# Attention and feed-forward in one kernel: the feed-forward steps two at a time, and x at another place in memory

## The chip, the cores and the metric

The kernel runs on one core of one Trainium2 chip. A core has a matrix engine (TensorE, PE in the profile), a vector engine (VectorE, DVE), a scalar engine (ScalarE, ACT), a general engine (GpSimd, POOL), and a sync engine (SyncE, SP) whose queue here issues every transfer. Each works through its own list of instructions in order; semaphores make one wait for another. The metric is the device time of one execution in microseconds (us), lower is better. A time is given as the median of several runs.

## What is computed

Four sequences of 768 tokens, eight heads of 64. Each query attends to the keys less than 16 places away and to 24 summaries, one for each block of 32 tokens: the maximum of the block's keys (its score raised by log 32), the mean of its values. The result, x with 512 features, goes through a feed-forward part with 2048 hidden features and a gate that is 0 below −1, h above 1 and (h + 1)²/4 between. Cut to what matters:

```python
k_sum = k.reshape(B, H, nb, block, D).max(axis=3)
v_sum = v.reshape(B, H, nb, block, D).mean(axis=3)
scores_l_m = np.where(mask_l, scale * q @ k.T, -1e9)
scores_s = scale * q @ k_sum.T + np.log(block)
a = softmax(concat([scores_l_m, scores_s]))
x = a @ concat([v, v_sum])
h = x @ w_in
g = np.where(h >= 1, h, np.where(h <= -1, 0.0, (h + 1) ** 2 / 4))
out = g @ w_out
```

## The kernel before

**Chunks, pairs and steps.** The 3072 tokens are cut into 8 chunks of 384, so a sequence is two chunks; an even chunk begins a sequence. Heads go in four pairs of 128 features. The hidden features go in 16 steps of 128 (f = 0 to 15). x, g and the two weights are each split into a high and a low half of a reduced 32-bit type (fp32r), and each product is made from three: low times high, high times low, high times high.

**A feed-forward step.** Step f of a chunk has these parts, with their letters in the code:
- F (`ff1`, L374): h, 12 products of 384 columns, whose moving operand is x. h takes one of two PSUM banks (`ps_h`).
- G, H (ACT, L380 and L386) and I (DVE, L392): the gate. I is the last reader of h and frees its bank.
- J (ACT, L397) and O (POOL, L402): the high and the low half of g. There are three buffers for the high and two for the low halves.
- B (`ff2`, L415): acc, 9 products of 512 columns, into three banks (one for each 128 tokens), over all 16 steps.
B of a step stands two steps behind its F.

**The attention between the steps.** While a chunk's 16 steps run, the attention of the next chunk is made, one pair of heads in each four steps. Ahead of every fourth step (`meet`): A, the values' product of one pair (o_ps, L350), its high and low halves X and L, then the next pair's S, the scores (s_ps, L292), mask, exponentials E and normalising. Behind the h of the last of four (`turn`): T, transposes (t_ps, L336), and P, their copies. Where the next chunk begins a sequence, the first turn of the chunk also makes Z (L267): one transpose of vsum, the sums of the values' blocks of all four pairs (vs_ps). V and W take it from there into the values.

**Loads and the shared buffers.** The raw values of a sequence (vraw, four loads of 384 KB, `load_raw_vals`, L221) are summed by DVE (Y, L249). The raw keys (kraw, L202) are reduced by DVE into ksum (R, L241). When a chunk is through, its result is copied from PSUM into three tiles o (U, L421 and L423) and stored (L427). vraw, kraw and o all have tag "w" of one pool, with three buffers in rotation: each new tile waits until the one three places earlier has been used up, a result tile's when its store has landed.

**The order.** Chunk 0 and the first few products of chunk 1 follow a list written out by hand (`OPENING`, L41 to L62). Chunks 1 to 7 follow a loop (L503 to L523) that fixes the order of PE by hand; the order of the other engines is put by a scheduler. In the loop before the change, a chunk begins: `meet`, B of step 14 of the chunk before, F of step 0, `finish` of the chunk before (B of its step 15, copies, stores), F 1, F 2, B 0, F 3, turn, B 1, and goes on with F f, B f − 2. In odd chunks the loads and sums of the next sequence's values stand in the loop ahead of F 0 (pairs 0 and 1) and ahead of F 1 (pairs 2 and 3).

**Small constants.** Three columns of constants (`ones_half`, `tiny`, `halved`) lie in spare columns of ksum.

Of the kernel before, what the change touches and what calls it, by code (L numbers as in the profile page):

```python
# [8 lines left out]
F32 = mybir.dt.float32  # L9
# [29 lines left out]
LAG = 2  # L39
# [36 lines left out]
def fused_kernel(ctx: ExitStack, tc: tile.TileContext, q2, kT, kwin, vT, vwin, w_in, w_out, mask, ident, out):  # L76
# [4 lines left out]
    stage = ctx.enter_context(tc.tile_pool(name="stage", bufs=1))  # L81
    load = ctx.enter_context(tc.tile_pool(name="load", bufs=2))
    att = ctx.enter_context(tc.tile_pool(name="att", bufs=2))
    xpool = ctx.enter_context(tc.tile_pool(name="xpool", bufs=2))
    gpool = ctx.enter_context(tc.tile_pool(name="gpool", bufs=3))
    ps_h = ctx.enter_context(tc.tile_pool(name="ps_h", bufs=2, space=PSUM))
    ps = ctx.enter_context(tc.tile_pool(name="ps", bufs=6, space=PSUM))

# [1 line left out]
    ident_sb = const.tile([P, P], F32, name="ident_sb")  # L90
    ident_up = const.tile([P, P], F32, name="ident_up") if MASK_PE else None
    ksum = const.tile([P, NPAIR, SB], F32, name="ksum")
    ones_half, tiny, halved = ksum[:, 0, NSUM:NSUM + 1], ksum[:, 0, NSUM + 1:NSUM + 2], ksum[:, 0, NSUM + 2:NSUM + 4]
    nc.vector.memset(ones_half, 0.5)
    nc.vector.memset(tiny, 1e-9)
    vsum = const.tile([P, NPAIR, SB], F32, name="vsum")
# [43 lines left out]
    def convert_join(i, at):  # L140

        step, part = divmod(at, 2)
        low, top = (word[:, part * DM:(part + 1) * DM] for word in raws[i])
        if step == 0:
            c_ps = joining[i, part] = ps.tile([P, DM], I32, tag="ps", name=f"c{i}_{part}")
            nc.vector.tensor_scalar(out=c_ps, in0=top, scalar1=3, scalar2=0x7FFFFFF8,
                                    op0=ALU.logical_shift_left, op1=ALU.bitwise_and)
        elif step == 1:
            nc.vector.scalar_tensor_tensor(out=joining[i, part], in0=top, scalar=-0x80000000, in1=joining[i, part],  # L149
                                           op0=ALU.bitwise_and, op1=ALU.bitwise_or)  # L150
        else:
            if i not in converting and i in LATE:
                converting[i] = room(i, "wide", [P, 4 * DM], F32)[:, :2 * DM].bitcast(I32)
                for n in range(2):
                    whole[pairs[i][1] + n] = converting[i][:, n * DM:(n + 1) * DM].bitcast(F32)
# [26 lines left out]
    q_ts, k_ts, v_ts, s_pss, es, dens, t_pss, pts, vs_pss, o_pss, xs = ({} for _ in range(11))  # L182
# [9 lines left out]
    for i, share in enumerate(FIRST):  # L192
        at, at_room = 0, room(NF - 1 - i, "first", [P, 4 * DM], F32)
        for what, p in share:
            shape = {"q": [NB, P], "k": [NB, KA], "v": [NB, P], "vraw": [S - T]}.get(what, [S])
# [20 lines left out]
    def load_raw_vals(c, p):  # L216


        first = T if c == 0 else 0
        v_raw = raws["v", c, p] = input_tile(stage, "vraw", [P, S - first], c, p)  # L220
        nc.sync.dma_start(out=v_raw, in_=vT[c // NHALF, p, :, first:])  # L221

    def load_vals(c, p):
        v_ts[c, p] = input_tile(load, "v", [P, NB, P], c, p)
# [19 lines left out]
        nc.gpsimd.tensor_copy(out=k_ts[c, p][:, :, KW:KA], in_=ksum[:, p, :NSUM].unsqueeze(1).broadcast_to([P, NB, NSUM]))  # L244

    def sum_vals(c, p):
        v_raw = raws["v", c, p]
        first = T // SB if c == 0 else 0
        nc.vector.tensor_reduce(out=vsum[:, p, first:NSUM], in_=v_raw.rearrange("p (n j) -> p n j", j=SB), axis=AX.X, op=ALU.add)  # L249
# [10 lines left out]
    def turn_vals(c, p):  # L260


        if c == 0:
            nc.tensor.transpose(vs_pss[c, p][:NSUM, P:2 * P], vsum[:, p, :NSUM], ident_sb)
        else:
            vs_pss[c, p] = ps.tile([P, 512], F32, tag="ps", name=f"vs_ps{c}_{p}")
            nc.tensor.transpose(vs_pss[c, p][:, :P], vsum.rearrange("p a b -> p (a b)"), ident_sb)  # L267

    def mean_vals(c, p):
# [75 lines left out]
    def values(c, p):  # L345
        o_pss[c, p] = ps.tile([P, 512], F32, tag="ps", name=f"o_ps{c}_{p}")
        for blk in range(NB):
            cols = slice(blk * QB, (blk + 1) * QB)
            for j in range(2):
                nc.tensor.matmul(o_pss[c, p][j * D:(j + 1) * D, cols], v_ts[c, p][:KA, blk, j * D:(j + 1) * D],  # L350
                                 pts[c, p, j][:KA, cols], start=True, stop=True)

    def high(c, p):
        hi = xpool.tile([P, T], F32R, tag=f"xhi{p}", name=f"xhi{c}_{p}")
        lo = xpool.tile([P, T], F32R, tag=f"xlo{p}", name=f"xlo{c}_{p}")
        if f"{c}{p}" in X_DVE:
# [12 lines left out]
    def ff1(c, f, k):  # L369
        if k == 0:  # L370
            hs[c, f] = ps_h.tile([P, 512], F32, tag="h", name=f"h{c}_{f}")
        x_hi, x_lo = xs[c, k]
        for n, (w, x) in enumerate(((1, x_hi), (0, x_lo), (0, x_hi))):
            nc.tensor.matmul(hs[c, f][:, :T], weight["win", f][w][:, k], x,  # L374
                             start=(k == 0 and n == 0), stop=(k == NK - 1 and n == 2))
# [28 lines left out]
    def ff2(c, f):  # L404
        if f == 0:
            acc[c] = [ps.tile([P, DM], F32, tag="ps", name=f"acc{c}_{i}") for i in range(NTT)]
        if c == 0 and f in whole:
            products = [(gs[c, f], whole[f])]
        else:
            (g_hi, g_lo), (w_hi, w_lo) = gs[c, f], weight["wout", f]  # L410
            products = [(g_lo, w_hi), (g_hi, w_lo), (g_hi, w_hi)]
        for i in range(NTT):
            rows = slice(i * P, (i + 1) * P)
            for n, (a, w) in enumerate(products):
                nc.tensor.matmul(acc[c][i], a[:, rows], w, start=(f == 0 and n == 0),  # L415
                                 stop=(f == NF - 1 and n == len(products) - 1))
# [34 lines left out]
    def scale_ident():  # L451
# [6 lines left out]
        "T": transposes, "P": turned, "Y": sum_vals, "z": halve_sum, "x": halve_copy, "Z": turn_vals, "V": mean_vals, "W": spread_vals, "A": values, "X": high, "L": low,  # L458
# [37 lines left out]
    def finish(c):  # L496
        do(f"B{c}{NF - 1:x} " + " ".join(f"U{c}{i} o{c}{i}" for i in range(NTT)))
# [89 lines left out]
```

## Time and profile before

| | |
|---|---|
| median of 3 runs | 657.88 us (656.59 to 659.27) |
| the profiled execution | 657.0 us |
| its span | 655.2 us |
| mean granted clock of TensorE | 0.992 of full |
| busy: PE, ACT, POOL, DVE | 97%, 56%, 40%, 38% |
| moved by DMA | 71.25 MB, 109 GB/s |

The page comes from one execution. Rows of groups give the line of the kernel, engine, operation, output and inputs, shapes, count, then busy microseconds, mean nanoseconds of one, and the idle time ahead of them with what ended it. Rows of the timeline give start and duration in microseconds and then the same names; in brackets, if the engine stood idle before, how long and for whom. Matmuls are pipelined: a product's own duration is longer than the distance to the next, so lengths of runs are read from starts. "SPq" rows are the issue of transfers, and their duration is not that of the transfer.

### The profile page before, as it was taken

How to read it: one execution, taken by the hardware profiler on the slowest of the kernel's cores; microseconds unless marked ns; L12 is line 12 of the kernel's file. 1: busy time of each engine (PE TensorE's matmuls, PEld its weight loads, DVE VectorE, ACT ScalarE, POOL GpSimd, SP SyncE). 2: the span in 40 equal slices, each digit the busy share in tenths (PEclk: the TensorE clock that was granted, in tenths of full speed). 3: DMA queues.
4: the chain of work that ended last, by engine and by line, in shares of the span. 5: the costliest groups of instructions: out<-in, count | busy, mean ns of one | idle time of the engine just before them, and what ended most of it. 6: DMA issues, size and time to landing. Idle time of an engine off the chain costs nothing.

```text
span 655.2 us, 11582 instructions
## 1 busy us (share of the span) xinstructions
PE 634.8 (97%) x4471; PEld 562.7 (86%) x4471; DVE 245.7 (38%) x473; ACT 364.8 (56%) x952; POOL 265.1 (40%) x302
## 2 busy tenths in 40 slices
PE   3999999899999999999999999999999999999997
PEld 2888888788889888888988888898888898889996
DVE  5789989452214222251222422143222222211111
ACT  5689986455455555455455544555554554544333
POOL 3579998252343332243333333234333333212221
PEclk9979999999999999999999999999999999999999
DMA  8996452542115222261223420163221110010001
GB/s 328 411 414 230 177 198 72 196 163 72 32 41 192 72 73 71 72 194 47 72 72 125 139 72 15 58 214 98 71 72 60 64 46 20 1 49 0 1 2 48
DMA packets 28167, 71.25 MB, mean 109 GB/s; under 512 B 2800, under 2 KB 3568, under 8 KB 28112
## 3 DMA queue, kind: packets, MB, share of 16 engines
q1 hardware_dynamic: 28112, 70.52, 30.7%
q8 instruction: 35, 0.57, 0.4%
q14 instruction: 20, 0.16, 0.1%
HBM read 64.21 MB, written 6.29 MB: 108 GB/s over the span
## 4 chain that ended last, share of the span: by engine, by line
PE 91%; DMA 2%; ACT 2%; DVE 1%; POOL 1%; SPq 1%; issue 1%; POOLq 0%; DVEq 0%; ACTq 0%
PE h L374 40%; PE acc L415 39%; PE o_ps L350 4%; PE s_ps L292 4%; PE t_ps L336 3%; DMA ident_sb<-in_ident 1%; DMA raw<-in_w_in 1%; PE vs_ps L255 1%; ACT t L380 0%; DVE c L149 0%; ACT e L318 0%; POOL v L276 0%; SPq L202 0%; DVE t L392 0%; ACT raw L138 0%
## 5 line engine op out<-in xcount | busy, mean ns | idle before, releaser
L374 PE MATMUL h<-xhi,halves 128*128 128x384 f32 x1024 | 285.6, 340 | 3.3 <-DVE t L392 3.3
L415 PE MATMUL acc<-halves,ghi 128*128 128x512 f32 x768 | 240.4, 394 | 0.0
L402 POOL TENSOR_TENSOR glo<-t,ghi 128x384 fp32r<-128x384 f32 x128 | 129.0, 1009 | 236.4 <-ACT ghi L397 236.4
L374 PEld LDWEIGHTS h<-xhi,halves 128*128 128x128 f32 x1024 | 187.6, 188 | 12.0 <-DVE t L392 4.4
L374 PE MATMUL h<-xlo,halves 128*128 128x384 f32 x512 | 172.1, 336 | 0.0
L392 DVE SCALAR_TENSOR_TENSOR t<-h,t 128x384 f32<-128x384 f32 x128 | 71.0, 556 | 264.8 <-ACT t L386 261.2
L415 PEld LDWEIGHTS acc<-halves,ghi 128*128 128x128 f32 x768 | 144.1, 188 | 27.9
L415 PE MATMUL acc<-halves,glo 128*128 128x512 f32 x384 | 153.2, 399 | 0.8 <-POOL glo L402 0.8
L380 ACT ACTIVATE t<-h,ksum 128x384 f32<-128x384 f32 x128 | 73.7, 578 | 118.0 <-PE h L374 116.3
L397 ACT CAST ghi<-t 128x384 fp32r<-128x384 f32 x128 | 65.6, 513 | 68.3 <-DVE t L392 68.2
L318 ACT ACTIVATE e<-e,den 128x120 f32<-128x120 f32 x192 | 73.2, 383 | 52.1 <-DVE den L307 52.0
L374 PEld LDWEIGHTS h<-xlo,halves 128*128 128x128 f32 x512 | 96.4, 188 | 4.0
L415 PEld LDWEIGHTS acc<-halves,glo 128*128 128x128 f32 x384 | 72.2, 188 | 13.7 <-POOL glo L402 1.5
L386 ACT ACTIVATE t<-t 128x384 f32<-128x384 f32 x128 | 66.8, 525 | 2.4
L331 POOL TENSOR_TENSOR e<-e,den 128x360 f32<-128x360 f32 x64 | 49.2, 787 | 41.0 <-DVE den L327 37.8
L276 POOL COPY v<-mean 24x768 f32<-24x768 f32 x30 | 24.7, 822 | 56.0 <-DMA v<-in_vwin 48.4
L179 POOL TENSOR_TENSOR halves<-w,halves 128x1024 fp32r<-128x1024 f32 x16 | 38.6, 2411 | 1.6 <-PE acc L415 0.5
L364 DVE TENSOR_TENSOR xlo<-o_ps,xhi 128x384 fp32r<-128x384 f32 x32 | 17.8, 556 | 49.1 <-ACT xhi L359 49.0
L318 ACT ACTIVATION_READ_ACCUMULATOR e<-e,den 128x1 f32 x192 | 36.0, 187 | 0.0
L350 PEld LDWEIGHTS o_ps<-pt,v 120*64 120x64 f32 x720 | 24.5, 143 | 10.7 <-issue 6.7
L303 DVE SCALAR_TENSOR_TENSOR e<-s_ps,mask_sb 128x360 f32<-128x360 f32 x64 | 30.9, 524 | 6.2 <-PE s_ps L292 5.9
L336 PE MATMUL t_ps<-ident_sb,e 128*120 128x128 f32 x192 | 29.7, 289 | 2.2 <-DMA ident_sb<-in_ident 2.1
(68 smaller groups left out, 405.9 us busy)
## 6 DMA issues: line engine op xcount, KB each, us to landing
v<-in_vwin SPq DMA_DIRECT2D x29, 384.0 KB, 3.2
q<-in_q SPq DMA_DIRECT2D x28, 384.0 KB, 4.2
k<-in_kwin SPq DMA_DIRECT2D x28, 360.0 KB, 4.6
raw<-in_w_in SPq DMA_DIRECT2D x8, 1024.0 KB, 9.7
raw<-in_w_out SPq DMA_DIRECT2D x8, 1024.0 KB, 13.2
out<-o SPq DMA_DIRECT2D x24, 256.0 KB, 2.0
kraw<-in_kT SPq DMA_DIRECT2D x13, 384.0 KB, 3.7
vraw<-in_vT SPq DMA_DIRECT2D x12, 384.0 KB, 3.7
```

The lines of the kernel that those rows point to most:

```text
L179: nc.gpsimd.tensor_tensor(out=lo, in0=converting[i].bitcast(F32), in1=hi.bitcast(F32), op=ALU.subtract)
L318: nc.scalar.activation(out=es[c, p, j][:, t, :], in_=s[:, t, :], func=AF.Exp, bias=nm[:, t:t + 1], scale=scale, accum_out=den[:, t:t + 1])
L331: nc.gpsimd.tensor_tensor(out=e, in0=e, in1=den.unsqueeze(2).broadcast_to([P, NT, KA]), op=ALU.mult)
L336: nc.tensor.transpose(t_pss[c, p, j][:KA, t * P:(t + 1) * P], es[c, p, j][:, t, :], ident_sb)
L350: nc.tensor.matmul(o_pss[c, p][j * D:(j + 1) * D, cols], v_ts[c, p][:KA, blk, j * D:(j + 1) * D], pts[c, p, j][:KA, cols], start=True, sto ...
L374: nc.tensor.matmul(hs[c, f][:, :T], weight["win", f][w][:, k], x, start=(k == 0 and n == 0), stop=(k == NK - 1 and n == 2))
L380: nc.scalar.activation(out=ts[c, f], in_=hs[c, f][:, :T], func=AF.Relu, bias=ones_half, scale=0.5)
L386: nc.scalar.square(out=ts[c, f], in_=ts[c, f])
L392: nc.vector.scalar_tensor_tensor(out=g, in0=hs[c, f][:, :T], scalar=1.0, in1=ts[c, f], op0=ALU.max, op1=ALU.min)
L397: nc.scalar.copy(out=hi, in_=ts[c, f])
L402: nc.gpsimd.tensor_tensor(out=lo, in0=ts[c, f], in1=hi.bitcast(F32), op=ALU.subtract)
L415: nc.tensor.matmul(acc[c][i], a[:, rows], w, start=(f == 0 and n == 0), stop=(f == NF - 1 and n == len(products) - 1))
```

## The change

**Pairs.** From chunk 1's loop on, PE makes two steps of h in a row (24 products), then two of acc (18 products). A group of four steps becomes meet, F F, B B, F F, turn, B B. A chunk begins: meet, B 14 and B 15 of the chunk before with its copies and stores, F 0, F 1, F 2, F 3, turn, B 0, B 1. The last chunk ends with four B in a row.

**The values' loads.** In odd chunks all four loads and sums of the next sequence's values stand behind F 1, and so behind `finish` with its three result tiles.

**Places.** The three constants move to a small tile of 64 bytes in `xpool`, and `gpool` is now created ahead of `xpool`. So the tiles of x lie 64 bytes into a block of 256; before they began such a block, as those of g and the weights did and do.

**The rest.** `full`, `X_POOL`, `F_DVE`, the key of `whole` and the full-length vraw tiles are not used by any step of this program or change no instruction, but for `HALF`, which keeps the shorter sums of chunk 0 as they were. The order of the hand-written list is unchanged on every engine.

```diff
+HALF = "02 00 01 03".split()
...
+    gpool = ctx.enter_context(tc.tile_pool(name="gpool", bufs=3))
     xpool = ctx.enter_context(tc.tile_pool(name="xpool", bufs=2))
-    gpool = ctx.enter_context(tc.tile_pool(name="gpool", bufs=3))
...
-    ones_half, tiny, halved = ksum[:, 0, NSUM:NSUM + 1], ksum[:, 0, NSUM + 1:NSUM + 2], ksum[:, 0, NSUM + 2:NSUM + 4]
+    small = xpool.tile([P, 16], F32, tag="small", name="small", bufs=1)
+    ones_half, tiny, halved = small[:, 0:1], small[:, 1:2], small[:, 2:4]
...
     with tc.manual_schedule(engines={mybir.EngineType.PE}):
         for c in range(1, NCH):
-            for f in range(NF):
+            for f in range(0, NF, 2):
                 if f % 4 == 0:
                     meet(c, NPAIR - 1) if f == 0 else meet(c + 1, f // 4 - 1)
-                    if f == 0:
-                        do(f"B{c - 1}{NF - LAG:x}")
-                s = f"{c}{f:x}"
-                if c % NHALF and c + 1 < NCH and f < 2:
-                    do(" ".join(f"y{c + 1}{p} Y{c + 1}{p}" for p in (2 * f, 2 * f + 1)))
+                if f == 0:
+                    do(f"B{c - 1}{NF - 2:x}")
+                    finish(c - 1)
+                for n in (f, f + 1):
+                    s = f"{c}{n:x}"
+                    do(f"F{s}0 F{s}1 F{s}2 F{s}3 G{s} H{s} I{s} J{s} O{s}")
+                if c % NHALF and c + 1 < NCH and f == 0:
+                    do(" ".join(f"y{c + 1}{p} Y{c + 1}{p}" for p in range(NPAIR)))
...
-                do(f"F{s}0 F{s}1 F{s}2 F{s}3 G{s} H{s} I{s} J{s} O{s}")
-                if f % 4 == 3 and c + 1 < NCH:
+                if f % 4 == 2 and c + 1 < NCH:
                     turn(c + 1, f // 4)
-                if f >= LAG:
-                    do(f"B{c}{f - LAG:x}")
-                elif f == 0:
-                    finish(c - 1)
-        do(f"B{NCH - 1}{NF - LAG:x}")
+                if f:
+                    do(f"B{c}{f - 2:x} B{c}{f - 1:x}")
+        do(f"B{NCH - 1}{NF - 2:x}")
         finish(NCH - 1)
```

What this does to the order is seen best at the start of chunk 3. In the names below, a number behind o is the tile of the result, behind vraw and kraw the pair of heads, behind t, h, glo and ghi the step, behind acc the bank; the last number tells tiles of one name apart. First SyncE's queue before the change:

```order
98 L427 DMA out<-o_0_3077 128x512
99 L427 DMA out<-o_1_3080 128x512
100 L427 DMA out<-o_2_3083 128x512
101 L221 DMA vraw_2_3086<-in_vT 128x768
102 L221 DMA vraw_3_3089<-in_vT 128x768
103 L202 DMA kraw_1_3183<-in_kT 128x768
```

And SyncE's queue at the same place after it:

```order
96 L448 DMA out<-o_0_3051 128x512
97 L448 DMA out<-o_1_3054 128x512
98 L448 DMA out<-o_2_3057 128x512
99 L228 DMA vraw_0_3102<-in_vT 128x768
100 L228 DMA vraw_1_3105<-in_vT 128x768
101 L228 DMA vraw_2_3108<-in_vT 128x768
102 L228 DMA vraw_3_3111<-in_vT 128x768
103 L209 DMA kraw_1_3172<-in_kT 128x768
```

The loads of vraw 0 and 1 stood in the chunk before (rows 84 and 85 of the queue) and now follow the three stores. VectorE in the same place before the change:

```order
284 L392 SCALAR_TENSOR_TENSOR t_0_3060<-h_0_3047,t_0_3060 128x384
285 L421 COPY o_1_3080<-acc_1_2356 128x512
286 L392 SCALAR_TENSOR_TENSOR t_1_3105<-h_1_3092,t_1_3105 128x384
287 L249 TENSOR_REDUCE vsum<-vraw_2_3086 128x24
288 L392 SCALAR_TENSOR_TENSOR t_2_3126<-h_2_3113,t_2_3126 128x384
289 L249 TENSOR_REDUCE vsum<-vraw_3_3089 128x24
```

And VectorE after it:

```order
283 L413 SCALAR_TENSOR_TENSOR t_0_3073<-h_0_3060,t_0_3073 128x384
284 L413 SCALAR_TENSOR_TENSOR t_1_3094<-h_1_3081,t_1_3094 128x384
285 L256 TENSOR_REDUCE vsum<-vraw_0_3102 128x24
286 L256 TENSOR_REDUCE vsum<-vraw_1_3105 128x24
287 L413 SCALAR_TENSOR_TENSOR t_2_3127<-h_2_3114,t_2_3127 128x384
288 L256 TENSOR_REDUCE vsum<-vraw_2_3108 128x24
289 L256 TENSOR_REDUCE vsum<-vraw_3_3111 128x24
290 L413 SCALAR_TENSOR_TENSOR t_3_3148<-h_3_3135,t_3_3148 128x384
```

All four sums now stand between the gates of steps 1 and 3. TensorE around the turn of the value sums before the change, from the last products of step 3's h on:

```order
1251 L374 MATMUL h_3_3146<-xhi_3_2995,halves_511 128x384
1252 L374 MATMUL h_3_3146<-xlo_3_2996,halves_511 128x384
1253 L374 MATMUL h_3_3146<-xhi_3_2995,halves_511 128x384
1254 L267 MATMUL vs_ps_0_3167<-ident_sb,vsum 128x128
1255 L336 MATMUL t_ps_0_0_3171<-ident_sb,e_0_0_3014 120x128 x3
1256 L336 MATMUL t_ps_0_1_3177<-ident_sb,e_0_1_3016 120x128 x3
1257 L415 MATMUL acc_0_3134<-halves_578,glo_1_3110 128x512
```

And TensorE after it:

```order
1245 L395 MATMUL h_3_3135<-xhi_3_2996,halves_512 128x384
1246 L395 MATMUL h_3_3135<-xlo_3_2997,halves_512 128x384
1247 L395 MATMUL h_3_3135<-xhi_3_2996,halves_512 128x384
1248 L275 MATMUL vs_ps_0_3156<-ident_sb,vsum 128x128
1249 L344 MATMUL t_ps_0_0_3160<-ident_sb,e_0_0_3015 120x128 x3
1250 L344 MATMUL t_ps_0_1_3166<-ident_sb,e_0_1_3017 120x128 x3
1251 L436 MATMUL acc_0_3180<-halves_579,glo_0_3078 128x512
```

Behind the turn there now stands acc of step 0 (glo_0), and step 1 behind it; before, step 0 was ahead of step 3's h.

More of the change, by code (lines that the diff above doesn't have):

```diff
@@ L68 @@
 X_DVE = "10 11 12 13".split()
+X_POOL = "".split()
+F_DVE = "".split()
 A_POOL = "".split()
+HALF = "02 00 01 03".split()
 MASK_PE = "".split()
@@ L153, in convert_join @@
                 converting[i] = room(i, "wide", [P, 4 * DM], F32)[:, :2 * DM].bitcast(I32)
+                name, f = pairs[i]
+                wide = converting[i].bitcast(F32)
                 for n in range(2):
-                    whole[pairs[i][1] + n] = converting[i][:, n * DM:(n + 1) * DM].bitcast(F32)
+                    whole[name, f + n] = (wide.rearrange("p (c t n) -> p c t n", c=NK, t=2)[:, :, n] if name == "win"
+                                          else wide[:, n * DM:(n + 1) * DM])
             elif i not in converting:
@@ L179, in convert_rest @@
         nc.gpsimd.tensor_tensor(out=lo, in0=converting[i].bitcast(F32), in1=hi.bitcast(F32), op=ALU.subtract)
-    q_ts, k_ts, v_ts, s_pss, es, dens, t_pss, pts, vs_pss, o_pss, xs = ({} for _ in range(11))
+    q_ts, k_ts, v_ts, s_pss, es, dens, t_pss, pts, vs_pss, o_pss, xs, fulls = ({} for _ in range(12))
     def input_tile(pool, what, shape, c, p):
@@ L194, in fused_kernel @@
         for what, p in share:
-            shape = {"q": [NB, P], "k": [NB, KA], "v": [NB, P], "vraw": [S - T]}.get(what, [S])
+            shape = {"q": [NB, P], "k": [NB, KA], "v": [NB, P]}.get(what, [S])
             flat = at_room[:, at:at + math.prod(shape)]
@@ L216, in load_raw_vals @@
     def load_raw_vals(c, p):
-        first = T if c == 0 else 0
-        v_raw = raws["v", c, p] = input_tile(stage, "vraw", [P, S - first], c, p)
-        nc.sync.dma_start(out=v_raw, in_=vT[c // NHALF, p, :, first:])
+        first = T if f"{c}{p}" in HALF else 0
+        v_raw = raws["v", c, p] = input_tile(stage, "vraw", [P, S], c, p)
+        nc.sync.dma_start(out=v_raw[:, first:], in_=vT[c // NHALF, p, :, first:])
     def load_vals(c, p):
@@ L246, in sum_vals @@
     def sum_vals(c, p):
-        v_raw = raws["v", c, p]
-        first = T // SB if c == 0 else 0
-        nc.vector.tensor_reduce(out=vsum[:, p, first:NSUM], in_=v_raw.rearrange("p (n j) -> p n j", j=SB), axis=AX.X, op=ALU.add)
+        v_raw = raws["v", c, p].rearrange("p (n j) -> p n j", j=SB)
+        first = T // SB if f"{c}{p}" in HALF else 0
+        nc.vector.tensor_reduce(out=vsum[:, p, first:NSUM], in_=v_raw[:, first:], axis=AX.X, op=ALU.add)
     def halve_sum(c, p):
@@ L260, in turn_vals @@
     def turn_vals(c, p):
+        if f"{c}{p}" not in HALF:
+            vs_pss[c, p] = ps.tile([P, 512], F32, tag="ps", name=f"vs_ps{c}_{p}")
         if c == 0:
@@ L265, in turn_vals @@
         else:
-            vs_pss[c, p] = ps.tile([P, 512], F32, tag="ps", name=f"vs_ps{c}_{p}")
             nc.tensor.transpose(vs_pss[c, p][:, :P], vsum.rearrange("p a b -> p (a b)"), ident_sb)
@@ L351, in values, with full @@
                                  pts[c, p, j][:KA, cols], start=True, stop=True)
+    def full(c, p):
+        fulls[c, p] = xpool.tile([P, T], F32, tag=f"xlo{p}", name=f"x{c}_{p}")
+        if f"{c}{p}" in F_DVE:
+            nc.vector.tensor_copy(out=fulls[c, p], in_=o_pss[c, p][:, :T])
+        else:
+            nc.scalar.copy(out=fulls[c, p], in_=o_pss[c, p][:, :T])
     def high(c, p):
@@ L355, in high @@
         lo = xpool.tile([P, T], F32R, tag=f"xlo{p}", name=f"xlo{c}_{p}")
-        if f"{c}{p}" in X_DVE:
+        if f"{c}{p}" in X_POOL:
+            nc.gpsimd.tensor_copy(out=hi, in_=fulls[c, p])
+        elif f"{c}{p}" in X_DVE:
             nc.vector.tensor_copy(out=hi, in_=o_pss[c, p][:, :T])
@@ L371, in ff1 @@
             hs[c, f] = ps_h.tile([P, 512], F32, tag="h", name=f"h{c}_{f}")
[L372 to L375, printed above, removed]
+        if c == 0 and ("win", f) in whole:
+            products = [(whole["win", f], fulls[c, k])]
+        else:
+            (x_hi, x_lo), (w_hi, w_lo) = xs[c, k], weight["win", f]
+            products = [(w_lo, x_hi), (w_hi, x_lo), (w_hi, x_hi)]
+        for n, (w, x) in enumerate(products):
+            nc.tensor.matmul(hs[c, f][:, :T], w[:, k], x, start=(k == 0 and n == 0),
+                             stop=(k == NK - 1 and n == len(products) - 1))
     def gate_half(c, f):
@@ L406, in ff2 @@
             acc[c] = [ps.tile([P, DM], F32, tag="ps", name=f"acc{c}_{i}") for i in range(NTT)]
-        if c == 0 and f in whole:
-            products = [(gs[c, f], whole[f])]
+        if c == 0 and ("wout", f) in whole:
+            products = [(gs[c, f], whole["wout", f])]
         else:
@@ L457, in fused_kernel @@
         "K": window_keys, "R": sum_keys, "C": summary_keys, "S": scores, "M": masks, "E": exps, "i": guards, "D": reciprocals, "N": norms,
-        "T": transposes, "P": turned, "Y": sum_vals, "z": halve_sum, "x": halve_copy, "Z": turn_vals, "V": mean_vals, "W": spread_vals, "A": values, "X": high, "L": low,
+        "T": transposes, "P": turned, "Y": sum_vals, "z": halve_sum, "x": halve_copy, "Z": turn_vals, "V": mean_vals, "W": spread_vals, "A": values, "f": full, "X": high, "L": low,
         "a": convert_top, "b": convert_low, "c": convert_join, "j": move_whole, "d": convert_high, "e": convert_rest,
```

## The prediction

> **What bounds the kernel now.** I read the busy times, then the chain of work that ended last, then the costliest groups.
>
> ```profile
> PE 634.8 (97%) x4471; PEld 562.7 (86%) x4471; DVE 245.7 (38%) x473; ACT 364.8 (56%) x952; POOL 265.1 (40%) x302
> PE 91%; DMA 2%; ACT 2%; DVE 1%; POOL 1%; SPq 1%; issue 1%; POOLq 0%; DVEq 0%; ACTq 0%
> L374 PE MATMUL h<-xhi,halves 128*128 128x384 f32 x1024 | 285.6, 340 | 3.3 <-DVE t L392 3.3
> L415 PE MATMUL acc<-halves,ghi 128*128 128x512 f32 x768 | 240.4, 394 | 0.0
> ```
>
> TensorE (PE) is busy for 97% of the span and carries 91% of the chain; in front of the products it stands idle for 3.3 us in all. So only two things move the time: how closely the products follow each other, and any moment in which PE must wait. The change touches both at the start of a chunk. Times below count from the start of the first acc run of chunk 3 ("step 14" of chunk 2, at 273.39). The timeline of PE there, in order: step 14, h of step 0, acc of step 15, h of steps 1 and 2, acc of step 0, h of step 3, the turn of the value sums (vs_ps), acc of step 1. Columns: start, duration.
>
> ```profile
> 273.39 0.50 PE L415 MATMUL acc<-halves,glo 128*128 128x512 f32 x1
> 275.57 0.33 PE L374 MATMUL h<-xhi,halves 128*128 128x384 f32 x1
> 277.68 0.39 PE L415 MATMUL acc<-halves,glo 128*128 128x512 f32 x1
> 279.76 0.33 PE L374 MATMUL h<-xhi,halves 128*128 128x384 f32 x1
> 283.94 0.39 PE L415 MATMUL acc<-halves,glo 128*128 128x512 f32 x1
> 286.02 0.33 PE L374 MATMUL h<-xhi,halves 128*128 128x384 f32 x1
> 288.31 0.33 PE L267 MATMUL vs_ps<-ident_sb,vsum 128*128 128x128 f32 x1
> 289.05 0.48 PE L415 MATMUL acc<-halves,glo 128*128 128x512 f32 x1
> ```
>
> One step of h takes 2.11 us (275.57 to 277.68), one of acc 2.08 (277.68 to 279.76). The turn begins at +14.92, and only after the last sum of values on VectorE (DVE). What leads to that, on SyncE's queue (SPq), DVE and ScalarE (ACT):
>
> ```profile
> 279.57 1.63 SPq L427 DMA_DIRECT2D out<-o  x3
> 281.88 2.33 SPq L221 DMA_DIRECT2D vraw<-in_vT  x2
> 285.40 0.95 DVE L249 TENSOR_REDUCE vsum<-vraw 128x24 f32<-128x768 f32 x1 [1.48 <-DMA vraw<-in_vT]
> 287.30 0.95 DVE L249 TENSOR_REDUCE vsum<-vraw 128x24 f32<-128x768 f32 x1 [0.48 <-DMA vraw<-in_vT]
> 277.56 0.30 ACT L323 ACTIVATE den<-den,ksum 128x6 f32<-128x6 f32 x1
> 278.98 0.57 ACT L423 COPY o<-acc 128x512 f32<-128x512 f32 x1
> ```
>
> Here the result is copied, stored 0.59 us after its copy's start, a load of vraw takes the buffer 2.31 later (the store has to land), lands after 3.52, and is summed in 0.95. Only two of four loads go this way; the other two were made in the chunk before.
>
> **Part by part: the pairs.** A pair of steps is one run of 24 or 18 products. Steps 1 and 2 of h in a row already exist: 279.76 to 283.94 is 4.18, against twice 2.11. For acc the last run of the kernel shows it:
>
> ```profile
> 645.28 0.39 PE L415 MATMUL acc<-halves,glo 128*128 128x512 f32 x1
> ...
> 647.36 0.39 PE L415 MATMUL acc<-halves,glo 128*128 128x512 f32 x1
> ...
> 649.40 0.39 PE L415 MATMUL acc<-halves,glo 128*128 128x512 f32 x1
> ```
>
> The first nine take 2.08, the next nine 2.04. So a pair saves 0.03 to 0.04 of settling; four steps make two pairs of each kind, 0.14. There are 28 such groups in chunks 1 to 7; three of them end in a wait that swallows the saving (below). 25 × 0.14 = **−3.5 us**. No other rearranged product costs anything: their number is the same.
>
> **Two banks of h.** Chunks 2 to 7 now begin with four steps of h in a row. Step 2 needs the bank that step 0's minimum on DVE frees. The path from the end of h to that:
>
> ```profile
> 282.12 0.58 ACT L380 ACTIVATE t<-h,ksum 128x384 f32<-128x384 f32 x1 [1.35 <-PE h L374]
> 283.36 0.56 DVE L392 SCALAR_TENSOR_TENSOR t<-h,t 128x384 f32<-128x384 f32 x1 [3.03 <-ACT t L386]
> 283.95 0.51 ACT L397 CAST ghi<-t 128x384 fp32r<-128x384 f32 x1 [0.69 <-DVE t L392]
> 284.37 0.58 ACT L380 ACTIVATE t<-h,ksum 128x384 f32<-128x384 f32 x1
> ```
>
> Step 1's h ended at about 281.86, its minimum at 283.92: 2.06, as long as the step of h (2.08 behind another) that now covers it. With signal and restart I take 0.15 for step 2. For step 3 the next activation also stands behind the cast of step 0 on ACT (0.42 apart here), about 0.16 more. 0.31 a chunk in chunks 2, 4, 6 and 7: **+1.2 us**, bounds 0 (the cover just holds) and 2.4 (twice that).
>
> **All four loads behind the stores.** This decides. In odd chunks the loads and sums of the next sequence's values now all stand behind the result tiles; they share three buffers. The chain in chunk 3, by the durations above: step 15 of acc follows step 14 at once and ends at +4.22 (2.18 + 2.04). ACT is free of exponentials at +4.17 (277.56), copies the first result, the store is issued at +4.76, vraw 0's load 2.31 later at +7.07; it lands at +10.6. DVE takes the minima of steps 0 and 1 first, and the latter ends at about +10.6 too: h of step 1 ends at +8.41, and 2.06 and 0.16 follow. Sum 0 ends at +11.5. The fourth load needs sum 0's buffer: issued at +11.53, landed after 3.52 at +15.05, summed at +16.0, turn at **+16.06**. PE has ended h of step 3 at about +13.0 and stands idle for 3 us. Behind the turn in PE's order stand acc of steps 0 and 1; before, step 0 was done by then. So the loss is 16.06 − 14.92 = 1.14, and one step of acc, nine products of 0.227, 2.05: **+3.19**. In chunk 5:
>
> ```profile
> 427.35 0.50 PE L415 MATMUL acc<-halves,glo 128*128 128x512 f32 x1
> ...
> 442.09 0.27 PE L267 MATMUL vs_ps<-ident_sb,vsum 128*128 128x128 f32 x1
> ...
> 440.73 0.95 DVE L249 TENSOR_REDUCE vsum<-vraw 128x24 f32<-128x768 f32 x1 [0.60 <-DMA vraw<-in_vT]
> ```
>
> The turn was at +14.74, so 1.32 + 2.05 = **+3.37**. In chunk 1 all four loads were behind the stores before, too:
>
> ```profile
> 126.99 1.80 DVE L249 TENSOR_REDUCE vsum<-vraw 128x24 f32<-128x768 f32 x2
> ...
> 132.85 0.95 DVE L249 TENSOR_REDUCE vsum<-vraw 128x24 f32<-128x768 f32 x1 [0.94 <-DMA vraw<-in_vT]
> ...
> 127.96 0.33 SPq L221 DMA_DIRECT2D vraw<-in_vT  x1
> ...
> 134.39 0.27 PE L267 MATMUL vs_ps<-ident_sb,vsum 128*128 128x128 f32 x1
> ```
>
> Sum 0 comes one minimum (0.55) later, so the load issued at 127.96 goes at about 128.5, lands at 133.4 as late as before, and the turn stays at 134.35; acc of step 0 is still to do: **+2.05** (bounds 1.5 and 3.1).
>
> The loads' own bounds: the page's medians and the shortest.
>
> ```profile
> vraw<-in_vT SPq DMA_DIRECT2D x12, 384.0 KB, 3.7
> out<-o SPq DMA_DIRECT2D x24, 256.0 KB, 2.0
> DMA to landing us min/median/max: 2.8/3.8/7.7
> ```
>
> I take chunk 3's own 2.31 and 3.52, the latter between the medians 3.7 and 3.8 and the least; a median load would add 0.3 to each of three turns, and the shortest ones are a rival below.
>
> What else queues behind these loads on SP (keys of pairs 1 to 3, the next values and queries) goes about 1.1 us later. The keys of pair 1 are next needed by the scores behind acc of steps 0 and 1, 4.1 us behind the turn; that covers it, and without cover it would cost the 1.1. On ACT the cast of step 3 now waits for acc of step 0 to free its buffer; the copies for the turn stand ahead of it, and its consumer comes six microseconds later. These edits: 0.
>
> **The place of x.** x moves from 0 to 64 bytes into a block of 256; each of 1536 h products streams it. No row of this kernel has an fp32r product with another offset. Nearest are the score products, whose moving keys lie 480 bytes apart and so at many offsets:
>
> ```profile
> L292 PE MATMUL s_ps<-k,q x672: 262/263/313, 44.4 to 561.7; 64*64 64x120 f32 x168
> ```
>
> Least and median differ by 1 ns, so I take **0**. Bounds: steady h products follow at about 173 ns (2.08 / 12), acc ones at 227 (2.04 / 9); the 53 between them for 128 columns leaves 13 that don't grow with the columns. All of that gone would be −20 us; the slowest start of a run, 185 ns, on every product, +18. The Trainium skill (TensorE: Matmul & The Clock Gate, section "Back-to-back issue gap") gives N/2.4 + 2.5 ns for an isolated product behind another, 162.5 at 384 columns: by that page an estimate of −16 us if the offset alone brought this pitch, and no run here shows that it does.
>
> **Sum**: −3.5 + 1.2 + 2.05 + 3.19 + 3.37 + 0 = +6.3. The profiled execution took 657.0 us (span 655.2), so 663.3; the median of the runs shown is 657.88, 0.9 higher, and by it **664.2**.
>
> **The rivals.** *The clock falls in the new idle (13%).* The stretches in which PE did little, with its busy time and granted clock (1.00 or 0.50, ahead of the DMA share):
>
> ```profile
> 26.84:30.25 3.41, 2.39 (x22) 1.88 (x23) 3.41 (x10) 3.41 (x10) 2.46 (x4) 1.00 1.05 407
> 30.25:33.66 3.41, 3.41 (x35) 3.17 (x34) 3.41 (x8) 3.26 (x13) 3.08 (x2) 0.50 1.03 407
> 125.81:129.22 3.41, 2.09 (x12) 2.04 (x12) 3.41 (x6) 3.10 (x15) 0.15 (x1) 1.00 0.89 319
> ...
> 127.13 0.44 PE L374 MATMUL h<-xhi,halves 128*128 128x384 f32 x1 [2.40 <-DVE t L392]
> ```
>
> After the first the clock was halved; around the third, with an idle of 2.40 ahead of the product at 127.13, it was not. The 3 us of idle to come are between; a halved window of 3.41 loses 1.7, three of them 5.1: 669.3. The Trainium skill (the same page, section "Part 1: The HAM clock gate") has the clock fall after an idle window of about 3.4 us; by that rule the 2.4 us above are too short, as the trace shows, and 3 us would be, too.
>
> *The place of x makes each h product shorter (25%).* The forecast's loss is gone at 6.3 / 1536 = 4.1 ns each; with half of the 13 ns the sum is −4, 654; with all of it, 644. That is the case on the other side, faster from 6.2 ns on (3.3 us more). For it: the 13 ns are there in every product. Against it: the score row. I give 15% to faster, 10% to a gain that only cancels the loss.
>
> *The loads are as quick as their shortest (13%).* With 2.0 for a store and 2.8 for a load, sum 0 still waits for the minimum until +10.6; the fourth load lands at +14.33, the turn is at +15.33. The three terms become 2.46 (0.41 + 2.05), 2.64 and, at its bound, 1.5; with the banks at their bound 0 the sum is 6.6 − 3.5 = +3.1: 661.0, no difference that can be told.
>
> **The numbers.** About 0.5% (3.3 us) is what a measurement of this kernel can tell from no change. The forecast has 49%: alone it spans 661.6 to 669. Slower: 49 + 13 = 62%; same: 10 + 13 = 23%; faster: 15%. The range leaves out the stronger half of the gains (below 654.5) and the worst of the clock's case (above 670.5).
>
> **What would show it.** In the changed profile: PE idle for about 3 us before the turn in chunks 3 and 5 and less in chunk 1, put down to DVE's vsum; the turn 16 us after acc of step 14; the four vraw loads behind three stores; waits of about 0.15 for the minimum at steps 2 and 3; 24 products of h in about 4.18. Wrong it would be if those 24 took under 4.1 (the place of x), or if the turn came without idle.

## The result and the profile after

The changed kernel takes 665.68 us (median of 4 runs, 663.75 to 666.53), the kernel before 657.24 beside it: 1.012 times as long, 95% interval 1.009 to 1.015. The forecast was 664.2. The two profiled spans are 663.6 and 655.2 us. Single executions far above the others (1251 to 3498 us, in the last round of runs) are left out of every median here.

The page of the changed kernel: busy times, the granted clock in 40 slices, and the shares of the chain that ended last. The last line is the clock of the kernel before.

```profile
PE 636.8 (96%) x4471; PEld 565.5 (85%) x4471; DVE 246.1 (37%) x473; ACT 357.7 (54%) x952; POOL 266.1 (40%) x302
PEclk9999999899999999989999999998999999999999
PE 82%; POOL 5%; DMA 4%; issue 3%; DVE 3%; ACT 1%; SPq 1%; POOLq 0%; DVEq 0%; ACTq 0%
...
PEclk9979999999999999999999999999999999999999
```

PE's share of the chain fell from 91% to 82%, and the clock shows three dips, in chunks 1, 3 and 5, that the kernel before does not have. (The one dip of the kernel before lies in the opening; up to the first scores of chunk 1 the two kernels differ by 0.07 us.) The waits of PE name the place (total, times, longest, us):

```profile
PE vs_ps L275 <- DVE vsum L256: 8.2, 3, 3.9
...
PE h L395 <- DVE t L413: 2.9, 2, 2.4
```

Three turns wait 8.2 us for the value sums. The start of chunk 3 on PE, from acc of step 14 at 274.82: first products of acc, h and the turn, and of h the products by which the two steps that wait can be seen.

```profile
274.04 0.85 PE L300 MATMUL s_ps<-k,q 64*64 64x120 f32 x24
274.82 0.50 PE L436 MATMUL acc<-halves,glo 128*128 128x512 f32 x1
...
279.03 0.34 PE L395 MATMUL h<-xhi,halves 128*128 128x384 f32 x1
...
282.84 0.34 PE L395 MATMUL h<-xlo,halves 128*128 128x384 f32 x1
283.50 0.34 PE L395 MATMUL h<-xlo,halves 128*128 128x384 f32 x1
...
285.06 0.34 PE L395 MATMUL h<-xlo,halves 128*128 128x384 f32 x1
285.75 0.34 PE L395 MATMUL h<-xlo,halves 128*128 128x384 f32 x1
...
287.48 0.34 PE L395 MATMUL h<-xhi,halves 128*128 128x384 f32 x1
291.69 0.44 PE L275 MATMUL vs_ps<-ident_sb,vsum 128*128 128x128 f32 x1 [3.86 <-DVE vsum L256]
293.06 0.78 PE L436 MATMUL acc<-halves,glo 128*128 128x512 f32 x1
...
295.91 0.40 PE L436 MATMUL acc<-halves,glo 128*128 128x512 f32 x1
298.91 0.85 PE L300 MATMUL s_ps<-k,q 64*64 64x120 f32 x24
```

The reader sees the four steps of h end at +13.0 as worked out (287.48 is the last product), the two small waits between steps (0.66 and 0.69 us from one low product to the next instead of 0.52), the turn at +16.87, and acc of step 0 taking 2.85 us (293.06 to 295.91) instead of 2.05. The chain to the turn, on SyncE's queue and VectorE:

```profile
279.46 1.31 SPq L448 DMA_DIRECT2D out<-o  x3
282.93 4.37 SPq L228 DMA_DIRECT2D vraw<-in_vT  x4
285.99 1.98 DVE L256 TENSOR_REDUCE vsum<-vraw 128x24 f32<-128x768 f32 x2 [0.57 <-DMA vraw<-in_vT]
290.59 0.95 DVE L256 TENSOR_REDUCE vsum<-vraw 128x24 f32<-128x768 f32 x1 [1.30 <-DMA vraw<-in_vT]
```

And why acc of step 0 is slow: stretches of 3.41 us around the idle times of chunks 3 and 5. The columns are the length, the busy time of PE, PEld, DVE, ACT and POOL (with the number of instructions), the granted clock, the DMA share and GB/s.

```profile
287.72:291.13 3.41, 0.10 (x1) 0.00 (x0) 2.11 (x4) 1.52 (x3) 0.00 (x0) 1.00 0.82 245
291.13:294.54 3.41, 2.85 (x11) 2.60 (x12) 2.69 (x4) 1.24 (x3) 1.86 (x3) 0.50 0.64 215
444.73:448.14 3.41, 1.30 (x8) 0.98 (x6) 2.54 (x4) 2.00 (x4) 0.55 (x1) 1.00 0.75 228
448.14:451.55 3.41, 2.84 (x11) 2.59 (x12) 2.79 (x4) 1.24 (x3) 1.84 (x3) 0.50 0.69 240
```

After each idle stretch one stretch runs at half clock.

**Where the time went.** The start of the scores (s_ps) marks each group of four steps, so groups can be compared. In the kernel before, a group takes 19.21 us, for instance

```profile
292.14 0.84 PE L292 MATMUL s_ps<-k,q 64*64 64x120 f32 x24
311.35 0.84 PE L292 MATMUL s_ps<-k,q 64*64 64x120 f32 x24
```

and in the changed one 19.00 (298.91 to 317.91). The whole difference of the two profiled executions:

| groups | before | after | difference |
|---|---|---|---|
| all up to chunk 1's first (start of scores) | 123.89 | 123.96 | +0.07 |
| first of chunk 1 | 14.30 | 16.74 | +2.44 |
| first of chunk 3 | 19.53 | 24.87 | +5.34 |
| first of chunk 5 | 19.27 | 23.69 | +4.42 |
| first of chunks 2, 4, 6 | 19.20, 19.18, 19.20 | 19.33, 19.33, 19.34 | +0.42 |
| the other 17 | 19.21 | 19.00 | −3.46 |
| from the last scores to the end | 94.15 | 93.32 | −0.83 |

These add up to 8.40, by which the spans differ.

### The profile page after: what moved, and what is told of

The parts are those of the page before. It is cut to its first block, busy times and chain, and to the rows that moved or that the text cites. A ratio compares the mean times of both kernels' runs of the same rounds, so it can differ in the third digit from the quotient of the medians.

```text
span 663.6 us, 11682 instructions
## 1 busy us (share of the span) xinstructions
PE 636.8 (96%) x4471; PEld 565.5 (85%) x4471; DVE 246.1 (37%) x473; ACT 357.7 (54%) x952; POOL 266.1 (40%) x302
## 4 chain that ended last, share of the span: by engine, by line
PE 82%; POOL 5%; DMA 4%; issue 3%; DVE 3%; ACT 1%; SPq 1%; POOLq 0%; DVEq 0%; ACTq 0%
PE acc L436 36%; PE h L395 34%; PE o_ps L358 4%; PE t_ps L344 3%; PE s_ps L300 3%; DMA vraw<-in_vT 2%; POOL halves L186 2%; PE vs_ps L262 2%; DMA ident_sb<-in_ident 1%; POOL glo L423 1%; POOL halves L174 1%; DVE vsum L256 1%; POOL e L339 1%; DVE t L413 1%; DMA out<-o 1%
## 5 line engine op out<-in xcount | busy, mean ns | idle before, releaser
L395 PE MATMUL h<-xhi,halves 128*128 128x384 f32 x1024 | 278.4, 342 | 2.9 <-DVE t L413 2.9
L395 PEld LDWEIGHTS h<-xhi,halves 128*128 128x128 f32 x1024 | 187.5, 189 | 11.1 <-DVE t L413 6.1
L401 ACT ACTIVATE t<-h,small 128x384 f32<-128x384 f32 x128 | 73.4, 574 | 91.8 <-PE h L395 91.7
L376 ACT CAST xhi<-o_ps 128x384 fp32r<-128x384 f32 x28 | 13.4, 480 | 61.8 <-PE o_ps L358 61.8
L344 PE MATMUL t_ps<-ident_sb,e 128*120 128x128 f32 x192 | 31.4, 301 | 2.3 <-DMA ident_sb<-in_ident 2.0
```

The lines of the kernel that those rows point to most:

```text
L344: nc.tensor.transpose(t_pss[c, p, j][:KA, t * P:(t + 1) * P], es[c, p, j][:, t, :], ident_sb)
L395: nc.tensor.matmul(hs[c, f][:, :T], w[:, k], x, start=(k == 0 and n == 0), stop=(k == NK - 1 and n == len(products) - 1))
L401: nc.scalar.activation(out=ts[c, f], in_=hs[c, f][:, :T], func=AF.Relu, bias=ones_half, scale=0.5)
```

## The experiments

**Early loads.** In odd chunks the loads and sums of pairs 0 and 1 go ahead of the result tiles again:

```diff
                     do(f"B{c - 1}{NF - 2:x}")
+                    if c % NHALF and c + 1 < NCH:
+                        do(" ".join(f"y{c + 1}{p} Y{c + 1}{p}" for p in range(2)))
                     finish(c - 1)
```

> The changed kernel, but in odd chunks the loads and sums of the values of pairs 0 and 1 stand ahead of the result copies again, as before the change; pairs 2 and 3 stay behind the two steps of h. Theory (the loss is the wait of the turn for value sums that stand behind the stores): in chunks 3 and 5 the last sum ends by about 13 us after acc of step 14, when h of step 3 ends; no idle and no halved clock there. Of the 12.2 us that the changed kernel loses in its three turns, those of chunk 3 (5.3) and chunk 5 (4.4) go but for 0.13 each: about -9.5, so about 656, 1 us below the kernel before. Chunk 1 is not touched and keeps its wait of 1.6 us. Rival (four steps of h in a row on two banks, or the pairing itself, cost the time): no change, about 665.7.

Measured: 654.86 us (0.997 of the kernel before, 0.995 to 0.999). The first groups of chunks 3 and 5 took 20.15 and 19.45 us instead of 24.87 and 23.69, the clock stayed full, and what is left of the wait:

```profile
PE vs_ps L275 <- DVE vsum L256: 1.8, 2, 1.3
```

This is the wait of chunk 1 and 0.5 in chunk 3. Of the 10.8 us between this kernel and the changed one 9.0 lie in these two groups: two loads' place in a queue. Another 1.8 lie in chunk 1. There the edit, too, moves two sums ahead of a minimum on VectorE; but the run that fills the idle time (below) keeps the changed kernel's order in chunk 1 and is as quick there (14.98 us against 14.96), so this order is not what made the 1.8. The rival (pairing or banks) is out: both are in this kernel.

**Early loads and a later turn.** In addition:

```diff
+                if f == 2 and c % NHALF:
+                    do(f"B{c}0")
                 if f % 4 == 2 and c + 1 < NCH:
                     turn(c + 1, f // 4)
```

> As the run with early loads, and in odd chunks the turn stands behind acc of step 0 (h of steps 0 to 3, acc 0, turn, acc 1). Theory: in chunk 1, too, 2.05 us of acc cover the wait of 1.64 for the value sums, so the three turns cost nothing and what is left is the gain of the pairs: about 654, 1.7 below the run with early loads and 0.5% below the kernel before. Rival (the wait of the turn is not what costs): no different from the changed kernel.

Measured: 653.03 us (0.993, 0.991 to 0.995). PE waits for no value sum in a loop's turn any more; a part comes back at the values' product behind the turn, which now has only one step of acc between:

```profile
PE o_ps L358 <- POOL v L284: 0.7, 1, 0.7
```

**A later turn only.** The loads stay behind the stores, the turn stands behind acc of step 0 (the second edit without the first).

> The changed kernel, whose loads stay behind the stores, but in odd chunks the turn stands behind acc of step 0. Theory: acc of step 0 (2.05) fills the idle time: the waits 1.64, 3.86 and 2.67 before the turn become 0, 1.8 and 0.6, and the clock stays full (-2.8): -1.64 - 2.05 - 2.05 - 2.8 = -8.5, less about 0.7 in each chunk for the values' product, whose values come later behind the turn: 657 to 659. If the clock falls still, 660 to 662. Rival (the loss lies in the loads themselves, not in what stands behind the turn): 665.7 less only the 1.64 of chunk 1.

Measured: 655.61 us, a little better than expected (0.998, 0.996 to 0.9998). The waits ahead of the turns are 2.0 us in two turns:

```profile
PE vs_ps L275 <- DVE vsum L256: 2.0, 2, 1.3
```

The clock stayed full in chunks 3 and 5, whose first groups took 20.92 and 20.32 us. So late loads by themselves cost some 2.6 us (against 653.03 with early ones); it is what stands behind the wait in PE's order, 2.05 us of acc that was ready, and the clock that make them dear.

**Busy while it waits.** The wait stays, but PE is given work:

```diff
+            for _ in range({4: 36, 6: 24}.get(c, 0)):
+                nc.tensor.transpose(vs_pss[c, p][:, P:2 * P], ident_sb, ident_sb)
             nc.tensor.transpose(vs_pss[c, p][:, :P], vsum.rearrange("p a b -> p (a b)"), ident_sb)
```

> The changed kernel with work put into PE's idle time ahead of the turn: 36 transposes of the identity in chunk 3 and 24 in chunk 5, into columns of the same bank that nobody reads (about 95 ns each, 3.4 and 2.3 us, ahead of the value sums' arrival in the changed kernel's trace). The turn itself comes no earlier. Theory (the clock falls because PE idles, and half of each window's remaining 2.85 us is lost): the clock stays full there, acc of step 0 takes 2.05 instead of 3.5, and -1.4 in each of two chunks makes -2.8: about 662.9. Rival (the clock falls for another reason, or its fall is hidden): unchanged, 665.7; and if the filling delays the turn, slower.

Measured: 660.39 us (1.004, 1.003 to 1.006). The stretches around the wait of chunk 3 in this kernel:

```profile
286.20:289.60 3.40, 3.40 (x33) 3.32 (x32) 2.40 (x4) 1.52 (x3) 0.00 (x0) 1.00 0.83 247
289.60:293.00 3.40, 3.40 (x20) 2.96 (x20) 2.23 (x4) 1.58 (x4) 1.84 (x3) 1.00 0.64 208
```

The clock stays full, and the groups take 23.43 and 22.20 us: 1.44 and 1.49 less than in the changed kernel, for work that computes nothing. The turn of chunk 3 comes 17.6 us behind the start of the scores in both, so this is the price of the clock, as expected. The whole run gained 5.3, more than these 2.9. In the profiled executions another 1.76 lies in chunk 1, which the edit doesn't touch. Its turn waits for the sum of the fourth load; the issue of this load and its sum, in the changed kernel and then in this one:

```profile
128.50 0.33 SPq L228 DMA_DIRECT2D vraw<-in_vT  x1
133.73 0.95 DVE L256 TENSOR_REDUCE vsum<-vraw 128x24 f32<-128x768 f32 x1 [0.72 <-DMA vraw<-in_vT]
...
128.13 0.33 SPq L228 DMA_DIRECT2D vraw<-in_vT  x1
131.61 0.95 DVE L256 TENSOR_REDUCE vsum<-vraw 128x24 f32<-128x768 f32 x1
```

From issue to sum went 5.23 us there and 3.48 here: the load landed 1.75 later, in the same order. The changed kernel's clock was halved in chunk 1, too (last section), but ahead of a wait for this load, so it did not set the turn.

**The changed kernel a second time.**

> The changed kernel unaltered, a second time. The run with the idle time filled was 5.3 us below it, of which 2.9 lie in chunks 3 and 5 as expected and 1.8 in chunk 1, which the filling does not touch. If that is chance between executions (the loads' landing and the clock in chunk 1), this run's chunk 1 may take any of 14.3 to 16.7 us for its first group, and its median may be 663 to 666; if the time is 660 to 661, the filling did less than 2.9 us.

Measured: 662.56, 664.14 and 664.74 us in three executions (1.011, 1.010 to 1.013). Its profile is of a fourth execution, of 2949 us, so chunk 1 can't be read from it. The runs of the changed kernel so lie between 662.6 and 666.5 and those with the filling between 658.4 and 661.8: the 2.9 are in that. What chunk 1 took in the executions without a profile is not shown. Over all other profiled runs its first group took 13.55 to 16.74 us, with the order at its turn, with the landing of the loads, and with the clock: it took 13.55 with the later turn only, at full clock, and 14.91 with early loads and a later turn, where a stretch was halved.

**x at 0.** The constants go back to ksum, so x begins a block of 256 bytes again:

```diff
-    small = xpool.tile([P, 16], F32, tag="small", name="small", bufs=1)
-    ones_half, tiny, halved = small[:, 0:1], small[:, 1:2], small[:, 2:4]
+    ones_half, tiny, halved = ksum[:, 0, NSUM:NSUM + 1], ksum[:, 0, NSUM + 1:NSUM + 2], ksum[:, 0, NSUM + 2:NSUM + 4]
```

> The changed kernel with the constants back in the spare columns of ksum, so that the tiles of x begin a block of 256 bytes again; the order of every engine is that of the changed kernel. Theory A (the place of x sets how the first products of a run settle): a run of 24 h products behind acc takes 4.186 us as before the change instead of 4.161, a run of 18 acc products behind h 4.12 instead of 4.09; four runs in each of 28 groups make about +2.5 to +3 us, 668. Rival B (the place does nothing, the settling follows from the pairing): 4.161 and 4.093 stay and the time is 665.7. Rival C of the prediction (the place shortens every product): 173 ns for a settled product becomes more, which the changed kernel's unchanged 173 speaks against.

Measured: 667.21 us (1.016, 1.014 to 1.019), 1.5 above the changed kernel. A group in this kernel:

```profile
299.14 0.85 PE L299 MATMUL s_ps<-k,q 64*64 64x120 f32 x24
318.22 0.85 PE L299 MATMUL s_ps<-k,q 64*64 64x120 f32 x24
```

19.08 us (19.07 in the mean): the order by itself brings 0.14 a group, the place of x 0.07. The run of 24 h products is back at 4.186 us, the run of 18 of acc at 4.121 (medians over chunks 2 to 7, from the starts of the products), as theory A has it.

**The kernel before with x at 64.** The two edits of the places, applied to the kernel before.

> The kernel before, with only the places changed: the constants in a tile of 64 bytes, x 64 bytes into a block of 256. Theory A: each run of 12 h products behind acc loses its 26 ns of settling (2.106 to about 2.08 us) and each run of 9 acc products behind h about 27 of 41; some 31 runs in each of 7 chunks make -5 to -6 us, about 651.5. Rival B: 657.2, no change.

Measured: 652.46 us (0.993, 0.990 to 0.996), theory A. At the start of chunk 3, acc of step 15, then h of step 1 behind it, and a group:

```profile
276.83 0.39 PE L416 MATMUL acc<-halves,glo 128*128 128x512 f32 x1
...
278.88 0.34 PE L375 MATMUL h<-xhi,halves 128*128 128x384 f32 x1
...
291.09 0.85 PE L293 MATMUL s_ps<-k,q 64*64 64x120 f32 x24
...
310.12 0.85 PE L293 MATMUL s_ps<-k,q 64*64 64x120 f32 x24
```

Nine products of acc take 2.05 us instead of 2.08, twelve of h 2.081 instead of 2.106, a group 19.03 instead of 19.21. A settled product takes what it took (173 ns, 227 ns). The place does by itself, with the order untouched, nearly all that place and pairs do together: 0.18 of the 0.21 us a group, where the pairs alone did 0.14.

**Other places.** The kernel before with a constants' tile of 128 bytes (x at 128), with x and g both at 64 (the pools in the old order, the constants' tile first), and with g alone at 64 (the tile in gpool).

> The kernel before with x 128 bytes into a block of 256 instead of 64 (a constants' tile of 128 bytes). If any place but the start of a block does it: 2.08 us for 12 h products behind acc and 2.05 for 9 acc products behind h as with 64, 652.5. If the distance matters: other numbers between 2.08 and 2.106, 2.05 and 2.081, and a time up to 657.5.

> The kernel before with x and g both 64 bytes into a block of 256 (w as it is, at 0). x is what TensorE streams for h, g what it loads as weights for acc, w_out what it streams for acc. If only the place of x counts: runs as with x at 64 alone, 2.081 us for 12 h products behind acc, 2.053 for 9 acc products behind h. If the distance of x from g counts: as before the change, 2.106 and 2.081.

> The kernel before with g alone 64 bytes into a block of 256, x at 0. If the place of x counts: 2.106 and 2.081 us, no change. If the distance from g counts: 2.081 and 2.053, as with x at 64.

Measured, medians over chunks 2 to 7 of runs that follow the other kind:

| x, g at | us | 12 of h | 9 of acc | a settled product of h, of acc |
|---|---|---|---|---|
| 0, 0 (before) | 657.2 | 2.106 | 2.081 | 173, 227 |
| 64, 0 | 652.46 | 2.081 | 2.053 | 173, 227 |
| 128, 0 | 655.33 | 2.105 | 2.055 | 175, 227 |
| 64, 64 | 657.82 | 2.084 | 2.097 | 173, 233 |
| 0, 64 | 659.69 | 2.100 | 2.100 | 173, 233 |

A group of the last kernel for comparison (19.30 us; 19.27 in the mean):

```profile
293.08 0.85 PE L293 MATMUL s_ps<-k,q 64*64 64x120 f32 x24
312.38 0.85 PE L293 MATMUL s_ps<-k,q 64*64 64x120 f32 x24
```

Neither of the simple rules holds. x at 64 makes h settle quickly whatever g does; acc settles quickly with x off 0, but only while g is at 0, and with g at 64 its products never come down to 227. That the two pools also changed their order is not it: the changed kernel with x at 0 has them in the new order and the lengths of the kernel before. What in the chip makes the difference stays open; only four other places were tried.

**Banks.** As the run with early loads, and in chunks 2, 4, 6 and 7 the two steps of acc that are left over stand between h of steps 1 and 2:

```diff
                 if f == 0:
+                    if c % NHALF == 0 or c + 1 == NCH:
+                        for n in (0, 1):
+                            do(f"F{c}{n}0 F{c}{n}1 F{c}{n}2 F{c}{n}3 G{c}{n} H{c}{n} I{c}{n} J{c}{n} O{c}{n}")
                     do(f"B{c - 1}{NF - 2:x}")
```

> As the run with early loads, and in chunks 2, 4, 6 and 7 the order at the start is h of steps 0 and 1, acc of steps 14 and 15, h of steps 2 and 3, so that 4.1 us of acc lie between h of step 1 and of step 2. Theory (two banks make steps 2 and 3 wait 0.14 and 0.17): the first groups of these chunks cost 0.33 less each, about -1.2 in all after 0.1 of added settling: 653.6 against 654.9; in the trace a group then takes 19.00 us as the later ones do, instead of 19.33. Rival (the wait is hidden, or the later copies of the result delay the next acc): no change or slower.

Measured: 653.35 us against 654.86 (of the kernel before 0.994 and 0.997, whose intervals 0.992 to 0.996 and 0.995 to 0.999 overlap); the trace tells it apart. The first group of chunk 4:

```profile
350.06 0.85 PE L300 MATMUL s_ps<-k,q 64*64 64x120 f32 x24
...
369.06 0.84 PE L300 MATMUL s_ps<-k,q 64*64 64x120 f32 x24
```

19.00 us; 19.33 with early loads alone. The wait for the banks is real and has the size expected.

**Pairs where they cost nothing.** The kernel before with x at 64, the old order in the first four steps of chunks 1, 3 and 5, pairs elsewhere, acc of steps 14 and 15 behind h of steps 0 and 1 in the other chunks. The core of it:

```diff
+                if f < 4 and turns:
...
+                else:
+                    do(one)
+                    if f == 1:
+                        do(f"B{c - 1}{NF - LAG:x}")
+                        finish(c - 1)
+                    if f % 4 == 3 and c + 1 < NCH:
+                        turn(c + 1, f // 4)
+                    if f > 1 and f % 2:
+                        do(f"B{c}{f - 3:x} B{c}{f - 2:x}")
```

> The kernel before with x at 64 bytes; in the first four steps of chunks 1, 3 and 5 the order and the loads of before, pairs of steps everywhere else, with h of steps 0 and 1 ahead of acc of steps 14 and 15 in the other chunks. Theory: the steady groups take 19.00 us instead of 19.03 (x at 64 leaves the pairs almost nothing to save), the turns of chunks 1, 3 and 5 14.3, 19.3 and 19.2 as with x at 64 alone: 0.5 us below it, about 652.0, which the measurement can hardly tell from it. Rival (the pairs save their 0.14 a group beside the place): 649.

Measured: 651.16 us (0.992, 0.990 to 0.993), the fastest here and below both kernels. Its groups take 19.00 us, the turns cost nothing (first groups 14.28, 19.17, 19.17), as theory has it; against x at 64 alone (652.46) the difference is not certain, and the rival's 649 is out.

## Why the forecast held, point by point

The forecast was +6.3 us, measured were +8.4; the direction, the mechanism and its place were right. That the number came so near is in part luck: the clock, left out of the sum, cost 2.9, and the place of x, put at 0, brought back 1.5 to 2.

- **Pairs: −3.5 forecast.** The 0.14 a group was exact for the order alone (19.21 to 19.07, x at 0). The place of x added 0.07, so −0.20 in each of 25 groups, −5.0.
- **Two banks: +1.2 forecast.** Steps 2 and 3 waited 0.14 and 0.17 us where 0.15 and 0.16 were worked out; 0.33 a chunk, +1.3, undone by the run with the banks.
- **Chunk 5: turn at +16.06 forecast.** It came at +15.68: the fourth load was issued at +11.49 (forecast +11.53), but landed after 3.07 instead of 3.52.
- **Chunk 1: +2.05 forecast, +2.44 measured.** The fourth load was issued at 128.50 as forecast, and its sum began 5.23 us later, where 4.89 went by before. But this nearness holds for the profiled execution alone: with the same order the group took 14.98 us in the run with the filling, only 0.7 above the kernel before, and 16.13 with x at 0, 1.8 above it.
- **Chunk 3: turn at +16.06 forecast, +16.87 measured.** The term for the store was too small: from the first store's issue to the load that takes its buffer went 3.47 us (279.46 to 282.93) instead of 2.31, so the first load landed at +11.1, behind the minimum that was to hide it (ended at +10.6), and all that follows came 0.6 to 0.8 later.
- **The clock: a rival at 13%, wrongly kept out of the sum.** In the profiled execution it fell in chunks 3 and 5, at 1.44 and 1.49 us; the rival had 1.7. In chunk 1 it fell, too, at the idle time of 2.4 that the kernel before has as well, and ahead of a turn that waited for a load anyway. The step that failed is the comparison with a single idle time of 2.40 that had not brought it down. The Trainium skill (TensorE: Matmul & The Clock Gate, section "Part 1: The HAM clock gate") asks for an idle window of about 3.4 us; the measurement differs: in chunk 5, 2.67 us of idle time were enough, of which 2.11 lay in the stretch ahead of the halved one.
- **The place of x: 0 forecast.** It was worth 1.5 us within the change (by the medians; 25 × 0.07 makes 1.75) and 4.8 alone. The rival of the place priced it as so many nanoseconds on each of 1536 products; it is 25 to 28 ns on each run of products, in the first six of h and the first nine of acc. The row of score products, on which the 0 rested, could not show it: those are other products, in no such alternation.

So: 12.2 us lost in three turns (2.9 of it by the clock) and 1.3 at the banks, against 5.0 gained, 8.5 by these rounded terms and 8.4 by the spans. The waits of chunks 3 and 5, the clock, the banks and the place each have a run that undoes them; chunk 1's 2.4 and the landing of store and loads are read from rows of one execution.

## What to carry to other kernels

Where an engine works through a fixed order, ask of each wait not only how long it is but what ready work stands behind it: here two loads put behind three stores cost 9 us, and moving one ready step of acc ahead of the wait won back most of it with the loads as late as before. An idle time of TensorE can be paid for a second time in the clock: 2.67 us of it cost 1.49 more. And before an order is changed to save switches, try the places of the operands: 64 bytes saved 0.18 us a group with the order untouched, more than the pairs alone.

## What the runs showed of the hardware

In these traces the clock changes in steps of 3.41 us, and it goes by how busy PE was in one such stretch, not by the length of an idle time. Over all profiled runs, from chunk 1 on: after a stretch with PE busy for 0.43 of it or less the next was halved in all cases that can be seen but one, at 0.43 itself; after 0.49 or more at full clock never. The opening doesn't fit: there, in seven of the profiled runs, a stretch with 0.69 to 0.81 was followed by three halved ones, though PE was busy for 0.86 or more of each. In the kernel before 12 of the 22 products of that first stretch have two columns, and their records make up 1.47 of its 2.39 us; whether that is the reason is not shown. Chunk 1 shows why this looks like chance. Each kernel idles there for 2.4 us in the same place; in four profiled runs that fell within one stretch (PE busy for 0.30 of it), as here in the changed kernel,

```profile
123.88:127.29 3.41, 1.02 (x26) 0.71 (x25) 2.45 (x6) 2.89 (x9) 0.00 (x0) 1.00 0.83 263
127.29:130.70 3.41, 3.41 (x11) 3.41 (x12) 2.23 (x4) 2.37 (x11) 1.57 (x2) 0.50 0.85 300
```

and the next ran at half. In a fifth, with x at 128, 1.94 us of it did (busy 0.43), and the next was halved as well. In the others it lay across two with at most 1.75 us in one, as in the kernel before (PE busy for 2.33 and 2.09 of 3.41), and nothing happened. Once halved it took more to come back, in the one case that shows it: with x at 0, a stretch at half clock with PE busy for 0.66 of it was followed by another halved one.

```profile
289.49:292.91 3.42, 2.27 (x9) 2.20 (x10) 3.01 (x4) 1.24 (x3) 1.33 (x2) 0.50 0.82 257
292.91:296.32 3.41, 3.41 (x9) 2.65 (x9) 1.17 (x2) 0.07 (x1) 1.74 (x4) 0.50 0.09 34
```

The other surprise is that the place of an operand within 256 bytes changes the distance between fp32r products by some 6 ns (acc with g at 64: 233 instead of 227 ns) and the length of the settling behind a switch.
